# Inverse transform of a long convolution by four frequency tiles per token tile, in a fused SSM-convolution and GEGLU kernel on one core

## The chip, the core and the metric

The kernel runs on one core of a Trainium2 chip. The metric is device time of one execution in microseconds (us), the median of several runs. The core has five engines that run their own instruction streams in order: TensorE (PE, with its weight loads PEld), VectorE (DVE), ScalarE (ACT), GpSimd (POOL), and SyncE (SP), which here only issues DMAs. They wait for each other by semaphores.

## The reference

Two layers A and B, each applied twice, to 2048 tokens x 576 channels in bf16:

```python
def _A_ref(q, k, v, shift_k, ssm_k, ssm_D):
    # k_shift: causal 4-tap filter of k per channel
    kv = k_shift * v
    y = irfft(rfft(pad(kv, 2S)) * rfft(pad(ssm_k, 2S)))[:S]   # causal convolution of length S = 2048
    return q * (y + kv * ssm_D)
def _B_ref(x, w_gate, w_up, w_down):                            # 576 -> 4608 -> 576
    return (gelu(x @ w_gate) * (x @ w_up)) @ w_down

x = A_q
x = x + _A_ref(layernorm(x), A_k, A_v, ...)
x = x + _B_ref(layernorm(x), ...)
x = x + _A_ref(layernorm(x), A_k, A_v, ...)
x = x + _B_ref(layernorm(x), ...)
```

(The FFT calls are shortened here.) k, v and the filter are the same in both A layers, so y is computed once and used as a gate twice.

## The kernel before, in words

**The feed-forward part.** Tokens are cut into four chunks of 512. A *unit* is one B layer on one chunk; the eight units run in the passes [0], [1, 2], [3, 4], [5, 6], [7], and each pass goes through the 4608 hidden columns in three thirds. One unit in one third is a *visit*, so there are 24 visits, numbered here 0 to 23. A visit has a *gate/up phase* of 12 chunks (18 matmuls each, L1440, into one PSUM pair `gu`; ScalarE makes the gelu, L1444, and VectorE the product `hT`, L1445) and a *down phase* (4 token tiles of 24 matmuls, L1457, `dn`; VectorE adds the result to the residual, L1493, L1488 or L1479). Visit 0 runs in two token halves (L1365). PSUM has three rotating pairs for this (`psp`) and one for the convolution (`cps`). Chunk 2 (unit 4) needs the gate y of block 2 in visit 9, chunk 3 (unit 5) that of block 3 in visit 14, each to be ready for the next visit.

**The convolution.** The token axis is also cut into four blocks of 512. Block m's output is a sum over a of (transform of kv block a) x (transform of filter block m - a), transformed back, with half of each product sum carried over to the next block. A block has four *frequency tiles* kt of 128 and four *token tiles* mt of 128. With kt written as even or odd, and kt and kt + 2 added or subtracted, the transform splits into smaller ones.

- Forward (`quarter`, L228, pieces of two matmuls, L260): one token tile times its own two tables, ScalarE copies it out (L262), and VectorE puts the four together: `both` (L237 a float sum, L238 a float combination 2a - b), `odd` and `even` (L251, L243). Used for the filters and kv of blocks 2 and 3. The filter's pieces for block 3 wait for block 2's shifted pieces (`z_at`).
- Products (`v`, `prod`, L297 to L301) and their sums over a (`add`, L541 for the first two, L544 after that), in float, for each frequency tile and each part (real 0, imaginary 1). The float sums `zs` lie in four rotating `eo` buffers.
- `cross` (L315) adds and subtracts the sums of kt and kt + 2 into bf16 pieces (part, kt, sign); `shift` (L320) adds the former block's piece of the other part, which is the carry-over.
- `inverse` (L339): for one token tile, four pieces times four tables, in two column halves: 8 matmuls of 288 columns. ScalarE copies the tile out (L345).

The convolution's blocks 0 and 1 begin at the start, where TensorE has little else.

**What sets the order.** Everything is recorded by hand on a clock of the kernel's own (`Pace`: t.pe, t.dve, t.act, with constants such as C_PR or C_AC for costs). Between feed-forward matmuls `fill` takes VectorE steps from the queue `V` (or `U`, or the prologue steps `vq`) when their inputs are ready by that clock and they fit before a limit; `run_p` takes TensorE steps from `Pq`, in the down phase freely and in the gate/up phase only when the result is urgent. `run_loads` issues filter and kv loads on GpSimd's queue. Weight loads, and the transposes of the normalised activations `xn` into `xnT` (L1153), go through SP in the order in which the clock made them due. The instructions then run in that order on each engine, whatever the real times are.

**Both ends.** At the start, `begin` makes block 0's gate and the first activations: `head.gate` (L1291 and L1294), `head.norm` (L1244, with the statistic `rstd` from GpSimd, L1070), `head.turn` (transposes on TensorE, L1260) and `head.copy` (L1267), after which visit 0 starts. At the end, the last token tile's down product is made in two column halves, so that the first half's sum (L1466) and DMA (L1467) run while TensorE makes the second.

Of the kernel before, what the change touches and what calls it, by code (L numbers as in the profile page):

```python
# [16 lines left out]
ALU = mybir.AluOpType  # L17
F32 = mybir.dt.float32
BF16 = mybir.dt.bfloat16
# [3 lines left out]
P = 128  # L23
# [3 lines left out]
RT = BS // P  # L27
HW = 288
# [3 lines left out]
NEVER = 1e9  # L32
# [3 lines left out]
C_BF, C_TB, C_R4 = 0.41, 0.46, 0.77  # L36
C_SQ, C_TINY = 0.85, 0.6
N_KC, N_SM, N_EO, N_HR = 4, 4, 4, 3
C_AC, C_AB = 0.76, 0.76
C_TT, C_ST, C_BN, C_NORM, C_HT, C_GELU, C_EVA, C_EVD = 0.76, 0.82, 0.47, 0.62, 0.69, 0.6, 0.66, 0.76  # L40
LAG = 0.25
# [43 lines left out]
class Conv:  # L85
# [296 lines left out]
    def filt(self, b):  # L382
        nc, t, D = self.nc, self.t, self.D
        kc, own = {}, {}

        def load():
            own["t"] = self.kvp.tile([P, RT, D], BF16, tag="v", name="hT")
            nc.gpsimd.dma_start(out=own["t"][:], in_=self.Td[b].rearrange("(p i) d -> p i d", i=RT))
            own["at"] = t.pe + 9.0
        self.L.append((lambda: max(self.fwd_at.get(b - 1, NEVER), self.td_at.get(b, NEVER)), load))  # L390

        def out():
            if not kc:
                self.flush(NEVER)
                kc.update({k: self.kcp.tile([P, 2, D], BF16, tag="kc", name="hc") for k in range(RT)})
            return kc

        def seen(h):
            if h == 1:
                self.filt_at[b] = t.pe + 0.25  # L400

        def done(kt, h, when):
            if h == 1:
                for k in (kt, kt + 2):
                    self.spill(self.Hd[b][k], kc[k], when, (b, k))
        for h in range(2):
            self.Pq.extend(self.quarter(lambda: own["t"], out, h, lambda: max(own.get("at", NEVER), self.z_at[b - 1]()), seen, done))
        self.Pq.extend(self.then)
        self.then = []

    def step(self, m, kv=None, loaded=False):

        nc, D, t = self.nc, self.D, self.t
        kc, kr, hr, z, nyb, prs = {}, {}, {}, {}, {}, {}
        KTS = (0, 2, 1, 3)
# [30 lines left out]
            ready = get("k", "v") if need == "v" else get("k")  # L446
            self.V.append((ready, C_TT, run))

        pairs = [(kt, a) for kt in KTS for a in range(m + 1)]
        if m == 1:  # L450
            pairs = [(kt + (2 * e if a else 2 - 2 * e), a) for kt in range(2) for a in range(2) for e in range(2)]

# [15 lines left out]
                at[("ld", kt, a)] = t.pe + 9.0  # L468
            return run
        for kt, a in pairs:  # L470
            self.L.append((lambda a=a: max(self.hr_free[self.nhr % N_HR] if (m, a) != (1, 0) else 0.0,
                                           self.kr_free[self.nkr % 3] if a < m else 0.0,
                                           self.hd_at.get((m - a, kt), NEVER) if m - a > 1 else 0.0),
                           load(kt, a)))
# [23 lines left out]
        def out4():  # L498
            if not kc:
                self.flush(NEVER)  # L500
                kc.update({k: self.kcp.tile([P, 2, D], BF16, tag="kc", name="kc") for k in range(RT)})
            return kc

        def seen4(h):
# [10 lines left out]
        def v(kt, a, part):  # L515
            def run():
                K = kc[kt] if a == m else kr[(kt, a)][1]
                slot = None if a else self.npr % N_SM
                prs[(kt, a, part)] = (slot, self.prod(part, K, hr[(kt, a)][1], own=a > 0))
                if a == 0:  # L520
                    self.pr_free[slot] = NEVER

                def fin(when):
                    mark(("pr", kt, a, part), when + LAG)
                    if part == 1:
                        if hr[(kt, a)][0] is not None:
                            self.hr_free[hr[(kt, a)][0]] = when
                        if a < m:
                            self.kr_free[kr[(kt, a)][0]] = when
                return fin  # L530
            return run
        sums, zslot = {}, {}

        def add(kt, a, part):
            def run():
                slot, pr = prs[(kt, a, part)]
                if a == 1:
                    f, zslot[(kt, part)] = self.eo_tile("zs")
                    sums[(kt, part)] = f
                    slot0, pr0 = prs[(kt, 0, part)]  # L540
                    nc.vector.tensor_tensor(out=f[:], in0=self.halves(pr0[:]), in1=self.halves(pr[:]), op=ALU.add)  # L541
                else:
                    f = sums[(kt, part)]
                    nc.vector.tensor_tensor(out=f[:], in0=f[:], in1=self.halves(pr[:]), op=ALU.add)  # L544

                def fin(when):
                    if a == 1:
                        self.pr_free[slot0] = when
                return fin
            return run  # L550
# [13 lines left out]
        def shift(kt, part):  # L564
            def run():
                for sg in range(2):
                    z[(part, kt, sg)] = self.yb[(1 - part, kt, sg)]
                    self.shifted(nyb[(part, kt, sg)], z[(part, kt, sg)], part)
                return lambda when: mark(("z", kt, part), when + LAG)
            return run  # L570
        eo_done = get(*[("kc", kt, s, h) for kt in range(2) for s in range(2) for h in range(2)])
        for kt, a in pairs:
            for part in range(2):
                keys = [("ld", kt, a)] + ([("kc", kt % 2, s, h) for s in range(2) for h in range(2)] if a == m else [])
                self.V.append((lambda g=get(*keys), kt=kt, a=a: max(g(), 0.0 if a else self.pr_slot(),
                                                                     self.h1_at.get(kt, NEVER) if (m, a) == (1, 0) else 0.0), C_PR, v(kt, a, part)))
                if a > 0:
                    self.V.append((eo_done if a == 1 else lambda: 0.0, C_AC, add(kt, a, part)))
                if a == m and kt >= 2:
                    self.V.append((lambda: 0.0, 2 * C_AB, cross(kt - 2, part)))  # L580
                    self.V.append((lambda: 0.0, 2 * C_TB, shift(kt - 2, part)))
        for h in range(2):
            if h == 1 and m == 1:
                self.fresh = len(self.Pq)
                self.Pq.extend(self.between)
            if m > 1:
                self.Pq.extend(self.quarter(lambda: self.vt_[m], out4, h, get(("kv", h)), seen4, done4))
                continue
            for kt in range(2):
                for s in range(2):  # L590
                    self.Pq.append((lambda g=get(("kv", h)): max(g(), self.eo_slot()), 0.49, fwd(kt, s, h)))
        def inv(mt):
            def run():
                self.yb = nyb
                self.inverse(m, mt, self.terms(mt, z))
                done = t.on_act(C_EVA, t.pe + 0.98 + LAG)
                self.ps_free = done + LAG
                self.y_at[(m, mt)] = done + LAG
            return run
        zs = get(*[("z", kt, part) for kt in range(2) for part in range(2)])  # L600
        self.z_at[m] = zs
        out = [(lambda: max(zs(), self.y_used.get(m - 2, NEVER) if m > 1 else 0.0), 0.98, inv(mt), m) for mt in range(RT)]
        if m == 2:
            self.then = out
        else:
# [89 lines left out]
    def begin(self, head, tables):  # L695
# [4 lines left out]
        with ExitStack() as es:  # L700
# [134 lines left out]
                    self.prod(part, kc[kt], h0[kt], t[:])  # L835
                    A[(part, kt)] = t

            self.yb = {}

            def pair0(kt, sg):  # L840
                for part in range(2):
# [83 lines left out]
            head.norm(0)  # L925
            head.turn(0, 8)
            head.copy(0, nc.scalar.copy)
            head.gate(1, None, 0)
            head.norm(2)
            head.turn(2, 8, True)  # L930
            head.copy(2, nc.vector.tensor_copy, nc.scalar.copy)
            self.keep_y(0, 3, Y[3])
# [5 lines left out]
def ssm_geglu_kernel(ctx, tc, A_q, A_k, A_v, A_shift_k, A_ssm_k, A_ssm_D, B_x, B_w_gate, B_w_up,  # L938
# [296 lines left out]
    with tc.manual_schedule():  # L1235
# [162 lines left out]
        for wb, ph, ui, first, final in visits:  # L1398
# [50 lines left out]
                fill(t.pe + C_GU + (HURRY if hurry() else LEAD), now(), conv.left > 0)  # L1449
            for j in range(RT):  # L1450
                acc = psp.tile([P, 2, 512], F32, tag="pr", name="dn")
                xa = x_c[c][:, j, :]
                xh = xa.rearrange("p (h d) -> p h d", h=2)

                def down(fi, h):
                    at = AT0[j] if ui == 0 else j
                    nc.tensor.matmul(acc[:, h, 0:HW], lhsT=hT[:, fi, at * P:(at + 1) * P],  # L1457
                                     rhs=wd[2 * wb + fi // WT][:, fi % WT, h * HW:(h + 1) * HW],
                                     start=(fi == 0), stop=(fi == FP - 1))
                if wb == NWB - 1 and j == RT - 1:  # L1460
                    dst = out2[c * CH:(c + 1) * CH, :].rearrange("(p j) d -> p j d", j=RT)[:, j, :]
                    for h in range(2):
                        for fi in range(FP):
                            down(fi, h)
                        ob = work.tile([P, D], BF16, tag="ob", name="ob")
                        nc.vector.tensor_tensor(out=ob[:, 0:HW], in0=xh[:, h, :], in1=acc[:, h, 0:HW], op=ALU.add)  # L1466
                        nc.sync.dma_start(out=dst[:, h * HW:(h + 1) * HW], in_=ob[:, 0:HW])  # L1467
                    break
                for fi in range(FP):
# [78 lines left out]
```

## Time and profile before

| | us |
|---|---|
| median of 3 runs | 925.32 (925.19 to 926.32) |
| the profiled execution, its own time | 924.81 |
| its span in the profile | 923.0 |
| TensorE busy (matmuls) | 915.1 |
| VectorE busy | 592.1 |
| ScalarE busy | 291.6 |
| GpSimd busy | 143.4 |
| L1440, gate/up matmuls, 4968 | 541.5 |
| L1457, down matmuls, 2304 | 293.8 |
| L1445, hT on VectorE, 276 | 189.1 |

The span is what the profiler sees between the first and the last instruction; the execution's own time has 1.8 us around it. Matmuls are pipelined and a single one's length (376 ns for L1440) overlaps the next, so starts are compared, not lengths. VectorE is much fuller in the first half, where the convolution lies beside the feed-forward part: it is busy for 0.7 or more of each of the first 23 slices (a slice is a fortieth of the span) but one, and for 0.6 or less after that. TensorE is busy for 0.9 or more of every slice but the last.

### The profile page before, as it was taken

The numbers are of one execution on the slowest core, as the hardware profiler recorded it, in microseconds if no ns is written. First come the engines' busy times: TensorE is split into PE (matmuls) and PEld (weight loads), VectorE is DVE, ScalarE is ACT, GpSimd is POOL, SyncE is SP. The second block draws the span as 40 slices with busy tenths as digits, with TensorE's granted clock in tenths as the row PEclk, the third lists the DMA queues.
The fourth block names the chain that finished last, engine by engine and source line by source line (L and its number), as shares of the span: only waits on it lengthen the run. The fifth ranks groups of instructions, "written<-read, shape, count | busy, mean of one in ns | idle before, by whom it ended". The sixth has DMA issues, their size and how long they took to land.

```text
span 923.0 us, 19358 instructions
## 1 busy us (share of the span) xinstructions
PE 915.1 (99%) x8248; PEld 534.6 (58%) x8249; DVE 592.1 (64%) x1064; ACT 291.6 (32%) x538; POOL 143.4 (16%) x301
## 2 busy tenths in 40 slices
PE   9999999999999999999999999999999999999998
PEld 6786556465465565655655646646546556556555
DVE  8888977588888877888898864563333335433332
ACT  6663225433324234343123132341221224221211
POOL 2433004201113031320113101220000003000000
PEclk9999999999999999999999999999999999999999
DMA  9989977919528606963933901870820821977720
GB/s 257 344 204 255 176 185 149 257 40 250 176 89 181 199 10 107 271 129 70 264 100 82 227 31 36 164 162 1 154 78 1 155 78 21 166 176 171 141 61 26
DMA packets 128490, 130.25 MB, mean 141 GB/s; under 512 B 43538, under 2 KB 120339, under 8 KB 128404
## 3 DMA queue, kind: packets, MB, share of 16 engines
q1 hardware_dynamic: 119232, 93.47, 47.9%
q0 software_dynamic: 9168, 35.54, 11.8%
q8 instruction: 64, 1.05, 0.5%
q14 instruction: 22, 0.18, 0.1%
q10 hardware_dynamic: 4, 0.01, 0.0%
HBM read 107.76 MB, written 11.80 MB: 130 GB/s over the span
## 4 chain that ended last, share of the span: by engine, by line
PE 91%; DMA 5%; DVE 1%; SPq 1%; POOL 1%; issue 0%; ACT 0%; DVEq 0%; ACTq 0%
PE gu L1440 57%; PE dn L1457 29%; PE gu L1365 3%; DMA wgu<-in_B_w_up_dram 2%; PE cps L339 1%; DMA hn<-in_A_ssm_k_dram 1%; DMA hr<-Hd 1%; DMA Hd<-hc 1%; PE cps L260 1%; PE cps L222 1%; DMA k<-in_A_k_dram 0%; SPq L996 0%; POOL rstd L1070 0%; SPq L995 0%; ACT junk L1062 0%
## 5 line engine op out<-in xcount | busy, mean ns | idle before, releaser
L1440 PE MATMUL gu<-xnT,wgu 64*128 64x512 bf16 x4968 | 541.5, 376 | 0.4 <-DVE x_c L1488 0.4
L1440 PEld LDWEIGHTS <-wgu 64*128 64x128 bf16 x4968 | 240.6, 94 | 293.7 <-issue 7.5
L1444 ACT ACTIVATE ga<-gu 128x512 f32<-128x512 f32 x276 | 164.8, 597 | 510.5 <-PE gu L1440 501.9
L1445 DVE TENSOR_TENSOR hT<-ga,gu 128x512 bf16<-128x512 f32 x276 | 189.1, 686 | 201.7 <-ACT ga L1444 200.2
L1457 PE MATMUL dn<-wd,hT 128*128 128x288 bf16 x2304 | 293.8, 286 | 0.5 <-DVE ob L1466 0.5
L1457 PEld LDWEIGHTS <-hT 128*128 128x128 bf16 x2304 | 223.6, 98 | 66.1 <-issue 10.5
L1493 DVE TENSOR_TENSOR x_c<-x_c,dn 128x576 f32<-128x576 f32 x64 | 48.1, 752 | 57.8 <-PE dn L1457 57.6
L1054 POOL TENSOR_SCALAR nm<-s 128x1 f32<-128x1 f32 x58 | 22.3, 385 | 290.9 <-DVE x_c L1488 198.9
L1062 ACT ACTIVATE junk<-x_c,nm 128x576 bf16<-128x576 f32 x48 | 37.0, 770 | 30.2 <-POOL nm L1054 28.3
L1070 POOL TENSOR_TENSOR rstd<-ve,neghalf_t 128x1 f32<-128x1 f32 x62 | 41.5, 669 | 5.2
L467 POOL DMA_DIRECT2D hr<-Hd x32 | 17.4, 546 | 122.9 <-DVE prod L300 117.2
L262 ACT COPY eo<-cps 128x576 f32<-128x576 f32 x32 | 20.4, 637 | 36.3 <-PE cps L260 25.4
L1479 DVE TENSOR_TENSOR ob<-x_c,dn 128x576 bf16<-128x576 f32 x15 | 11.3, 753 | 29.3 <-PE dn L1457 22.7
L1365 PE MATMUL gu<-xnT,wgu 64*128 64x256 bf16 x432 | 24.7, 269 | 0.5 <-DMA wgu<-in_B_w_up_dram 0.5
L1069 POOL TENSOR_SCALAR ve<-ss 128x1 f32<-128x1 f32 x62 | 17.6, 285 | 42.0 <-ACT junk L1062 41.6
L1365 PEld LDWEIGHTS <-wgu 64*128 64x128 bf16 x432 | 21.2, 94 | 3.4 <-issue 0.7
L301 DVE TENSOR_TENSOR prod<-prod 128x576 bf16<-128x576 bf16 x48 | 22.0, 458 | 1.7
L354 POOL DMA_DIRECT2D out_dram<-ob x12 | 6.7, 555 | 95.7 <-DVE ob L1479 92.8
L544 DVE TENSOR_TENSOR zs<-zs,prod 128x576 f32<-128x576 f32 x24 | 18.1, 755 | 0.6
L541 DVE TENSOR_TENSOR zs<-sum,prod 128x576 f32<-128x576 bf16 x24 | 18.1, 755 | 0.4
L1097 DVE SCALAR_TENSOR_TENSOR x_c<-g_t,rstd,x_c 128x576 f32<-128x576 f32 x16 | 13.1, 817 | 8.2 <-POOL rstd L1070 8.1
L186 DVE TENSOR_TENSOR kvt<-k,skc 128x1152 bf16<-128x1152 bf16 x24 | 17.7, 753 | 0.2
(148 smaller groups left out, 543.7 us busy)
## 6 DMA issues: line engine op xcount, KB each, us to landing
wgu<-in_B_w_gate_dram SPq DMA_DIRECT2D x45, 576.0 KB, 5.8
wd<-in_B_w_down_dram SPq DMA_DIRECT2D x30, 864.0 KB, 7.1
wgu<-in_B_w_up_dram SPq DMA_DIRECT2D x45, 512.0 KB, 8.2
hr<-Hd POOLq DMA_DIRECT2D x32, 288.0 KB, 4.8
kr<-Kd POOLq DMA_DIRECT2D x24, 288.0 KB, 5.2
Kd<-kc POOLq DMA_DIRECT2D x12, 288.0 KB, 4.1
k<-in_A_k_dram POOLq DMA_DIRECT2D x3, 1008.0 KB, 10.5
wgu<-in_B_w_up_dram SPq DMA_DIRECT2D x45, 64.0 KB, 7.5
```

The lines of the kernel that those rows point to most:

```text
L262: nc.scalar.copy(out=A[i][:], in_=ps[:, :, 0:HW])
L301: nc.vector.tensor_tensor(out=dst, in0=pr[:, 0, :], in1=pr[:, 1, :], op=ALU.subtract if part == 0 else ALU.add)
L541: nc.vector.tensor_tensor(out=f[:], in0=self.halves(pr0[:]), in1=self.halves(pr[:]), op=ALU.add)
L1054: nc.gpsimd.tensor_scalar(out=v["nm"][:], in0=v["s"][:], scalar1=-1.0 / D, scalar2=None, op0=ALU.mult)
L1062: nc.scalar.activation(out=junk[:], in_=get_x(), func=ACT.Square, bias=v["nm"][:, 0:1], accum_out=v["ss"][:])
L1070: nc.gpsimd.tensor_tensor(out=v["rstd"][:], in0=ve[:], in1=neghalf_t[:, 0:1], op=ALU.pow)
L1365: nc.tensor.matmul(pair[:, s, e * 256:(e + 1) * 256], lhsT=w[r0:r0 + HK, k, gi * P:(gi + 1) * P], rhs=xnT[r0:r0 + HK, blk_of[k], tok], sta ...
L1440: nc.tensor.matmul(pair[:, s, :], lhsT=w[r0:r0 + HK, k, gi * P:(gi + 1) * P], rhs=xnT[r0:r0 + HK, b, :], start=(k == 0), stop=(k == NKC - 1))
L1444: nc.scalar.activation(out=ga[:], in_=pair[:, 0, :], func=ACT.Gelu_apprx_tanh)
L1445: nc.vector.tensor_tensor(out=hT[:, fi, :], in0=ga[:], in1=pair[:, 1, :], op=ALU.mult)
L1457: nc.tensor.matmul(acc[:, h, 0:HW], lhsT=hT[:, fi, at * P:(at + 1) * P], rhs=wd[2 * wb + fi // WT][:, fi % WT, h * HW:(h + 1) * HW], start ...
L1493: nc.vector.tensor_tensor(out=xh, in0=xh, in1=acc[:, :, 0:HW], op=ALU.add)
```

## The change

For blocks 2 and 3 (`quad`), the four frequency sums are put together on VectorE for each token tile before the tables, as the forward pieces already are, so that each token tile's inverse has two pieces instead of four. `halve` makes sum and difference of kt and kt + 2 in place, in float; `quart` adds or subtracts an even and an odd one into the bf16 piece of one token tile and part; `shift4` adds the carry-over per token tile. Since all four frequency sums have to be kept, those of odd kt lie in `kc` buffers instead of `eo` buffers, and for kt 3 the product with the block's own kv comes first so that its buffer is free in time. Block 1 leaves pieces of the old kind, which `convert` turns into the new kind, once. Each token tile's inverse waits for its own pieces alone. Block 2's inverse is put between the two halves of block 3's filter pieces instead of behind both. At the start, the normalisation of tile 2 stands ahead of the first half of tile 1's gate. At the end, the second column half has a PSUM tile of its own.

```diff
@@ filt
         for h in range(2):
             self.Pq.extend(self.quarter(...))
-        self.Pq.extend(self.then)
-        self.then = []
+            self.Pq.extend(self.then)
+            self.then = []
@@ step
-        pairs = [(kt, a) for kt in KTS for a in range(m + 1)]
+        quad = m > 1
+        seq = lambda kt: [m] + list(range(m)) if quad and kt == 3 else list(range(m + 1))
+        pairs = [(kt, a) for kt in KTS for a in seq(kt)]
@@ add
-                if a == 1:
-                    f, zslot[(kt, part)] = self.eo_tile("zs")
+                second = a == seq(kt)[1]
+                if second:
+                    if quad and kt % 2:
+                        self.flush(NEVER)
+                        f = self.kcp.tile([P, 2, HW], F32, tag="kc", name="zs")
+                    else:
+                        f, zslot[(kt, part)] = self.eo_tile("zs")
@@ new steps
+        def halve(kt, part):
+                lo, hi = sums[(kt, part)], sums[(kt + 2, part)]
+                nc.vector.tensor_tensor(out=hi[:], in0=lo[:], in1=hi[:], op=ALU.add)
+                nc.vector.scalar_tensor_tensor(out=lo[:], in0=lo[:], scalar=2.0, in1=hi[:], op0=ALU.mult, op1=ALU.subtract)
+        def quart(mt, part):
+                even = mt % 2 == 0
+                e, o = sums[(2 if even else 0, part)], sums[(3, part) if even else (1, 1 - part)]
+                minus = mt == 2 if even else (mt, part) in ((1, 0), (3, 1))
+                b = nyb[(mt, part)] = self.ybp.tile([P, D], BF16, tag="yb", name="yb")
+                nc.vector.tensor_tensor(out=self.halves(b[:]), in0=e[:], in1=o[:], op=ALU.subtract if minus else ALU.add)
+        def shift4(mt):
+                for part in range(2):
+                    z[(mt, part)] = self.yb[(mt, 1 - part)]
+                    self.shifted(nyb[(mt, part)], z[(mt, part)], part)
+        def convert(a, b, plus, minus):
+                lo, hi = self.yb[a], self.yb[b]
+                tmp = self.prp.tile([P, 2, D], BF16, tag="prod", name="prod")
+                nc.vector.tensor_tensor(out=tmp[:, 0, :], in0=lo[:], in1=hi[:], op=ALU.add)
+                nc.vector.tensor_tensor(out=hi[:], in0=lo[:], in1=hi[:], op=ALU.subtract)
+                nc.vector.tensor_copy(out=lo[:], in_=tmp[:, 0, :])
+                self.yb[plus], self.yb[minus] = lo, hi
@@ the queue of VectorE steps
+                if quad:
+                    if a == seq(kt)[-1] and kt >= 2:
+                        self.V.append((lambda: 0.0, 2 * C_AC, halve(kt - 2, part)))
+        if quad:
+            for mt in range(RT):
+                for part in range(2):
+                    self.V.append((lambda: 0.0, C_AB, quart(mt, part)))
+                self.V.append((lambda: 0.0, 2 * C_TB, shift4(mt)))
@@ inv
-                self.inverse(m, mt, self.terms(mt, z))
+                self.inverse(m, mt, [(self.inv_w(mt, s), z[(mt, s)]) for s in range(2)] if quad else self.terms(mt, z))
@@ begin
-            head.gate(1, None, 0)
             head.norm(2)
+            head.gate(1, None, 0)
             head.turn(2, 8, True)
@@ last token tile
+                last = wb == NWB - 1 and j == RT - 1
+                part = [acc, psp.tile([P, 2, 512], F32, tag="pr", name="dn") if last else acc]
-                    nc.tensor.matmul(acc[:, h, 0:HW], ...)
+                    nc.tensor.matmul(part[h][:, h, 0:HW], ...)
```

## The prediction on record

> **What bounds the kernel now.** I read the page first, then the chain, the waits of TensorE, its timeline around the inverses, and both ends.
>
> ```profile
> PE 915.1 (99%) x8248; PEld 534.6 (58%) x8249; DVE 592.1 (64%) x1064; ACT 291.6 (32%) x538; POOL 143.4 (16%) x301
> ...
> PE 91%; DMA 5%; DVE 1%; SPq 1%; POOL 1%; issue 0%; ACT 0%; DVEq 0%; ACTq 0%
> ```
>
> TensorE is busy 915.1 of 923.0 us and carries 91% of the chain. Its granted clock is 9 tenths or more in every slice. So a matmul taken away is worth its own length wherever nothing else becomes late. The waits (total, times, longest) say how little slack there is:
>
> ```profile
> PE xps L1260 <- DVE xn L1244: 0.8, 1, 0.8
> PE dn L1457 <- DVE ob L1466: 0.5, 1, 0.5
> ...
> PE gu L1440 <- DVE x_c L1488: 0.4, 1, 0.4
> ```
>
> Now the timeline of TensorE in visit 13 (block 3's inverse in the down phase), and after it that in visit 9 (block 2's fourth tile in the gate/up phase). First column start, second length; only starts are subtracted here, since ends are modelled.
>
> ```profile
> 550.76 1.14 PE L339 MATMUL cps<-yb,W 128*128 128x288 bf16 x8
> 551.74 1.39 PE L1457 MATMUL dn<-wd,hT 128*128 128x288 bf16 x10
> ```
>
> ```profile
> 382.81 9.89 PE L1440 MATMUL gu<-xnT,wgu 64*128 64x512 bf16 x90
> 392.62 1.16 PE L339 MATMUL cps<-yb,W 128*128 128x288 bf16 x8
> 393.71 13.77 PE L1440 MATMUL gu<-xnT,wgu 64*128 64x512 bf16 x126
> 407.42 0.42 PE L1457 MATMUL dn<-wd,hT 128*128 128x288 bf16 x2
> ```
>
> Among down matmuls, eight inverse matmuls take 551.74-550.76 = 0.98 us, 0.1225 each: no price for the interruption. Inside a gate/up phase the phase lasts 407.42-382.81 = 24.61 us, where an uninterrupted one has 23.42 in the chain: 1.19, so 0.21 on top of 0.98. I call that the switch.
>
> **The change part by part.** The execution profiled is 924.81 us (span 923.0); the sum is made against it.
>
> *The inverse.* Per token tile 8 matmuls become 4, on 2 blocks of 4 tiles: 32 matmuls x 0.1225 = **-3.92**. The order of the changed build shows the places. Before: seven of the eight groups among down matmuls, one in a gate/up phase. After: block 2's four among down matmuls of visit 8; block 3's, two among those of visit 13 and two in the gate/up phase of visit 14. A two-matmul filter piece also moves into visit 9's gate/up phase; such a piece costs there 23.89-23.42 = 0.47 (visit 5's phase, 235.84 to 259.73 in the chain), a switch of 0.22. So switches go from one to three: **+0.42**.
>
> *VectorE.* Per block it loses 8 of the 751 ns sums (L315) and gains 4 sums, 4 of the scaled kind (L238, 758 ns) and 8 sums: 8 more ops, 6.0 us a block, 12.1 in all. Block 1's pieces are converted once: 4 x (2 x 451 ns, as L320, and a copy). The trace has no 576-wide SBUF copy; 187 ns (64 wide) and 451 (a two-input op of that width) bound it. I take 250, nearer the 217 of the 256-wide copy: 4.6 us. None of it is on the path if VectorE fits. Visits 8 and 13 get most of it, since the rest of the work is moved into them. Counting the ordered ops there, visit 13 takes on 2+4+4 product ops, two first and two second sums, 4 halving and 7 quartering sums and 2 shifts, and loses 4 L315: 14.3 us by the rows' durations. It had 18.9 busy:
>
> ```profile
> 491.88:527.16 35.28, 35.28 (x314) 19.74 (x316) 31.00 (x55) 12.82 (x28) 10.06 (x19) 1.00 0.79 170
> 527.16:566.36 39.20, 39.20 (x346) 22.87 (x348) 18.91 (x31) 9.76 (x16) 1.62 (x3) 1.00 0.17 57
> ```
>
> (columns: stretch, length, then busy of PE, PEld, DVE, ACT, POOL.) Back-to-back ops start every 0.71 where one lasts 0.75, so 14.3 is about 13.5 of time: 32.4 in a visit of 39.20-2.94 = 36.3, or 0.89. Visit 12, the first row, ran at 31.00/35.28 = 0.88 with TensorE never idle. I take nothing; the third rival prices the loss of this cover.
>
> *Added waits.* Block 3's inverses now follow their shifts closely. From the start of visit 13's down phase, VectorE does the last hT (done at 1.4), a halving (2.9), a quarter, the output sum, a quarter and two shifts: 6.0. TensorE gets there after 54 matmuls, 6.6. The second tile: 9.0 against 9.8. Slack 0.6 to 0.8, cost nothing. Block 2's tiles are ready during visit 8's gate/up phase, so its wait ends earlier than before.
>
> *Queues.* Unit 5's last norm stands behind the last hT of visit 14, two chunks later than before. On SP a weight load is put ahead of three of its four pairs of transposes; it waits for the buffer that the phase's eighth chunk frees, and the second xn stands behind the ninth chunk's hT anyway. The last pair issues about 2.1 us into the down phase, takes 2 x 1.26, and lands 2.8 later: 7.4 of 11.9. POOL's filter loads only change places. I cost these at nothing; the slack of 4.5 is the cover.
>
> *The far end.* The second half's first matmul waits for a read of the same tile:
>
> ```profile
> 917.76 0.45 DVE L1466 TENSOR_TENSOR ob<-x_c,dn 128x288 bf16<-128x288 f32 x1 [0.72 <-PE dn L1457]
> ...
> 918.27 1.63 PE L1457 MATMUL dn<-wd,hT 128*128 128x288 bf16 x12 [0.55 <-DVE ob L1466]
> ```
>
> A tile of its own ends that: **-0.55**. What is late next is the second half itself; its sum and DMA follow unchanged.
>
> *The near end.* The gate step moves behind the norm of tile 2.
>
> ```profile
> 35.59 0.56 POOL L1070 TENSOR_TENSOR rstd<-ve,neghalf_t 128x1 f32<-128x1 f32 x1
> ...
> 36.89 0.81 DVE L1291 SCALAR_TENSOR_TENSOR x_c<-x_b,mv,y 128x576 f32<-128x576 bf16 x1
> 36.98 1.13 POOL L1070 TENSOR_TENSOR rstd<-ve,neghalf_t 128x1 f32<-128x1 f32 x1
> ...
> 38.15 0.58 DVE L1244 TENSOR_SCALAR xn<-x_c,nm,rstd 128x576 bf16<-128x576 f32 x1 [0.44 <-POOL rstd L1070]
> ```
>
> The norm waits for GpSimd's rstd, not for the gate step. But that rstd takes 1.13 beside the gate step and 0.56 the time before, and ends 0.41 after it. If it takes 0.56, xn starts at 37.6; the gate step then runs under the transposes, and VectorE's copy ends at 39.70 rather than 39.77, ScalarE's 0.57 earlier than 40.08. If it stays at 1.13, the gate step delays the copy to 40.24: +0.35. The chain names a weight DMA as the last releaser of the first gate/up matmul (39.87), but group 0's three loads landed 10 to 12 us after issues at 7 to 10, so I hold the copies to be last. I take **-0.2**, ends -0.3 and +0.35, by the 0.56 row.
>
> The Trainium skill, "SBUF — State Buffer", section "SBUF: two separate sides", says that VectorE ops with two SBUF inputs and GpSimd ops that read SBUF exclude each other for a whole instruction. By that rule the long rstd is the gate step's doing and this term is -0.2; without it, +0.35 and the sum 0.55 higher. The pair of rows agrees with it.
>
> **Sum:** -3.92 + 0.42 - 0.55 - 0.20 = **-4.25**, so 920.56 for an execution like the profiled one. That one lies 0.51 under the median of 925.32; I add it back: **921.1**.
>
> **Rivals.**
>
> 1. *VectorE late for the new waits.* For: four inverses have under 1 us of slack, and at the start of visit 8 (the L1488 wait above) VectorE waits in order for a chain through GpSimd. Against: block 1's inverses sat in a busy stretch without a wait. Two ops of 0.75 late, less 0.6 slack, is 0.9, at two places: +1.8, **922.9**.
>
> 2. *The gain is eaten: VectorE becomes the bound in visits 8 and 13.* For: the halvings, quarters and shifts come in dependent chains, and the order lets VectorE do little else between them. Against: 0.88 was borne without a wait. If only 0.83 can be filled, visit 13 needs 32.4/0.83 = 39.0 instead of 36.3, +2.7. Visit 8 goes by the same count from 27.87 to about 33.3, in 35.28 + 7 x 0.245 + 4 x 0.49 = 39.0; 33.3/0.83 = 40.1, +1.1. Sum +3.8: **924.9**, no change. (That the change does not do what it says is excluded by count: the build has 32 matmuls fewer.)
>
> 3. *Slower: unit 5's activations come late.* The place is the start of visit 15, the mechanism one chain: block 3's fourth inverse comes only after the seventh chunk of visit 14, then follow its copy, the last gate, three GpSimd steps and a square, and the last norm. The norm stands on VectorE ahead of the down phase's first sum (L1488), which frees a PSUM tile, and its transposes on SP ahead of a weight load. It decides from 4.5 us of slip. If the norm comes a whole down phase late, 11.9-4.5 = 7.4: **928.5**. Against: from the last gate (behind the eighth chunk's hT) to the norm there are four chunks, 7.8 us, where the same chain took 5.4 in visit 7 (337.24 to 342.63), with VectorE fuller.
>
> **How the numbers follow.** Forecast 0.76, rival one 0.11, two 0.08, three 0.05. The forecast's own ends: low 921.1-0.1 (near end) -0.4 (the L1488 wait also goes) -0.4 (no switch) -0.3 (median offset) = 919.9; high with +0.55 at the near end and the offset: 922. The range takes in the first rival and its doubt: **919.9 to 923.5**, leaving 0.13 out. About 0.2% (1.85 us) is what a measurement of this kernel can tell from no change, so faster means under 923.5: forecast and rival one, 0.87; same is rival two, 0.08; slower rival three, 0.05.
>
> **What would show it.** Right: L339 groups of four 0.49 long among down matmuls; visit 13 near 36.3 us; no wait for L1466; rstd 0.56 and an earlier first gate/up matmul; no new TensorE wait over 0.3. Wrong: a wait of L339 for shifted pieces or their copies (rival one), gate/up matmuls waiting for hT in visits 8 or 13 (two), a wait for xnT or wgu at visit 15 (three).

## The result, and the profile after

The changed kernel takes **919.99 us** (median, 919.81 to 920.6), the one before, run beside it, 925.73 (925.19 to 926.32). The ratio is 0.9939, with a 95% interval of 0.9922 to 0.9956, so the kernel is faster by 0.6%, clear of the noise. Forecast were 921.1 and a range of 919.9 to 923.5. The profiled execution took 919.96 us (span 917.8), against a sum of 920.56 for it.

In the changed kernel's listing the lines lie further down: gate/up matmuls are L1509 (before L1440), down matmuls L1528 (L1457), hT L1514 (L1445), the residual sums L1550, L1559 and L1564 (L1479, L1488 and L1493), visit 0's gate/up matmuls L1434 (L1365), the head's xn, copies and gate L1313, L1336 and L1360 (L1244, L1267 and L1291), rstd L1139 (L1070). New are `halve` (L583, L584), `quart` (L594) and `convert` (L618 to L620).

The page of the changed kernel: busy time and instructions of each engine, then the shares of the chain that ended last.

```profile
PE 911.2 (99%) x8217; PEld 530.0 (58%) x8217; DVE 607.5 (66%) x1092; ACT 291.5 (32%) x538; POOL 142.6 (16%) x301
...
PE 99%; ACT 0%; DVE 0%; DMA 0%; issue 0%; POOL 0%; DVEq 0%; ACTq 0%
```

TensorE has 31 recorded matmuls fewer (32 by the program; a record can be missing) and is busy 3.9 us less; VectorE is busy 15.4 us more. The mean granted clock is 1.0 in both profiled executions, so it plays no part in the difference.

The waits of TensorE (total us, times, longest):

```profile
PE ps L812 <- DVE full L795: 1.5, 1, 1.5
PE gu L1434 <- ACT xnT L1336: 0.8, 1, 0.8
PE ps L834 <- ACT skc L818: 0.5, 1, 0.5
PE cps L731 <- ACT kT L843: 0.3, 1, 0.3
PE xps L1329 <- DVE xn L1313: 0.2, 1, 0.2
PE ps L817 <- DMA sk<-in_A_shift_k_dram: 0.2, 1, 0.2
```

That is all that this view lists, and all of it lies in the head, ahead of visit 1 (it leaves out the shortest waits). The tail's wait for `ob` is gone, and so are two waits inside visits: the one of 0.4 for L1488 shown before, and one of 0.34 in visit 4 that I come to below. From visit 1 to the tail the view lists no wait of TensorE.

TensorE's timeline from visit 13's down phase to the end of visit 14's gate/up phase:

```profile
547.57 6.79 PE L1528 MATMUL dn<-wd,hT 128*128 128x288 bf16 x54
554.20 0.65 PE L339 MATMUL cps<-yb,W 128*128 128x288 bf16 x4
554.69 2.86 PE L1528 MATMUL dn<-wd,hT 128*128 128x288 bf16 x22
557.38 0.65 PE L339 MATMUL cps<-yb,W 128*128 128x288 bf16 x4
557.87 2.61 PE L1528 MATMUL dn<-wd,hT 128*128 128x288 bf16 x20
560.42 6.00 PE L1509 MATMUL gu<-xnT,wgu 64*128 64x512 bf16 x54
566.35 0.66 PE L339 MATMUL cps<-yb,W 128*128 128x288 bf16 x4
566.95 7.95 PE L1509 MATMUL gu<-xnT,wgu 64*128 64x512 bf16 x72
574.82 0.66 PE L339 MATMUL cps<-yb,W 128*128 128x288 bf16 x4
575.42 9.89 PE L1509 MATMUL gu<-xnT,wgu 64*128 64x512 bf16 x90
585.24 1.03 PE L1528 MATMUL dn<-wd,hT 128*128 128x288 bf16 x7
```

Four matmuls take 554.69-554.20 = 0.49 us among down matmuls, half of the 0.98 before. The gate/up phase lasts 585.24-560.42 = 24.82, which is 23.42 + 2 x 0.70: each of its two tiles costs 0.49 and a switch of 0.21, as in the forecast. No idle time stands beside any L339, so none of them waits.

Where the 4.85 us between the two profiled executions lie, by starts on TensorE:

| stretch | before | after | difference |
|---|---|---|---|
| to block 0's first inverse matmul (start of the run) | 29.52 | 29.99 | +0.47 |
| from there to visit 1 | 55.97 | 55.57 | -0.40 |
| visits 1 to 3 | 112.33 | 112.33 | 0 |
| visit 4 | 37.96 | 37.45 | -0.51 |
| visits 5 and 6 | 71.02 | 71.02 | 0 |
| visits 7 to 10 | 149.72 | 147.23 | -2.49 |
| visits 11 and 12 | 70.57 | 70.56 | -0.01 |
| visits 13 and 14 | 74.49 | 72.96 | -1.53 |
| visits 15 to 23, to the last down phase | 305.68 | 305.68 | 0 |
| last down phase to the last output sum | 12.68 | 11.97 | -0.71 |
| from there, and around the span | | | +0.33 |

The first row is scatter: it reads 29.52 to 30.45 in the traces of this study, and no edit touches what lies before it. The last row is mostly the time outside the span. That is 1.8 us in every execution of the kernel before and 2.1 in every one of the changed kernel, so it is no scatter; but e7 below, which has the same change, shows 1.8 in all ten of its executions, so the loss of 0.35 does not follow from the change as such, and what sets it stays open. Between these two rows the changed kernel gains 5.65 us. The medians stand 5.74 apart, with an interval of 4.1 to 7.2. Of visits 7 to 10, three tiles of the inverse account for 3 x -0.49, the fourth, moved from a gate/up phase to a down phase, for 0.49-1.19 = -0.70, the filter piece moved the other way for 0.45-0.245 = +0.20, and a wait gone in visit 8 for -0.53. So the inverse with its switches gives -1.97 there and -1.53 in visits 13 and 14: -3.5. Head -0.40, tail -0.71, and **-1.04 from two waits that I had left standing**.

### The profile page after: what moved, and what is told of

It reads as the page before. It is cut to its first block, busy times and chain, and to the rows that moved or that the text cites. A ratio compares the mean times of both kernels' runs of the same rounds, so it can differ in the third digit from the quotient of the medians.

```text
span 917.8 us, 19325 instructions
## 1 busy us (share of the span) xinstructions
PE 911.2 (99%) x8217; PEld 530.0 (58%) x8217; DVE 607.5 (66%) x1092; ACT 291.5 (32%) x538; POOL 142.6 (16%) x301
## 4 chain that ended last, share of the span: by engine, by line
PE 99%; ACT 0%; DVE 0%; DMA 0%; issue 0%; POOL 0%; DVEq 0%; ACTq 0%
PE gu L1509 59%; PE dn L1528 31%; PE gu L1434 3%; PE ps L211 1%; PE cps L339 1%; PE cps L260 1%; PE cps L222 1%; PE cps L211 1%; PE hps L870 0%; PE cps L731 0%; PE ps L339 0%; PE ps L222 0%; PE xps L1329 0%; PE ps L731 0%; PE ps L817 0%; DMA sk<-in_A_shift_k_dram 0%
## 5 line engine op out<-in xcount | busy, mean ns | idle before, releaser
L1509 PE MATMUL gu<-xnT,wgu 64*128 64x512 bf16 x4968 | 541.7, 376 | 0.0
L1509 PEld LDWEIGHTS <-wgu 64*128 64x128 bf16 x4968 | 239.2, 94 | 294.4 <-issue 7.4
L1514 DVE TENSOR_TENSOR hT<-ga,gu 128x512 bf16<-128x512 f32 x276 | 189.1, 685 | 195.1 <-ACT ga L1513 193.2
L1528 PE MATMUL dn<-wd,hT 128*128 128x288 bf16 x2304 | 293.3, 286 | 0.0
L1528 PEld LDWEIGHTS <-hT 128*128 128x128 bf16 x2304 | 223.5, 98 | 65.4 <-issue 9.8
L1564 DVE TENSOR_TENSOR x_c<-x_c,dn 128x576 f32<-128x576 f32 x64 | 48.1, 752 | 60.6 <-PE dn L1528 60.2
L1139 POOL TENSOR_TENSOR rstd<-ve,neghalf_t 128x1 f32<-128x1 f32 x62 | 40.8, 658 | 5.2
L1434 PE MATMUL gu<-xnT,wgu 64*128 64x256 bf16 x432 | 24.6, 269 | 0.8 <-ACT xnT L1336 0.8
L1434 PEld LDWEIGHTS <-wgu 64*128 64x128 bf16 x432 | 21.1, 94 | 3.7 <-DMA wgu<-in_B_w_up_dram 0.9
L1550 DVE TENSOR_TENSOR ob<-x_c,dn 128x576 bf16<-128x576 f32 x15 | 11.3, 753 | 18.0 <-PE dn L1528 12.6
```

The source lines that it names most:

```text
L1139: nc.gpsimd.tensor_tensor(out=v["rstd"][:], in0=ve[:], in1=neghalf_t[:, 0:1], op=ALU.pow)
L1434: nc.tensor.matmul(pair[:, s, e * 256:(e + 1) * 256], lhsT=w[r0:r0 + HK, k, gi * P:(gi + 1) * P], rhs=xnT[r0:r0 + HK, blk_of[k], tok], sta ...
L1509: nc.tensor.matmul(pair[:, s, :], lhsT=w[r0:r0 + HK, k, gi * P:(gi + 1) * P], rhs=xnT[r0:r0 + HK, b, :], start=(k == 0), stop=(k == NKC - 1))
L1514: nc.vector.tensor_tensor(out=hT[:, fi, :], in0=ga[:], in1=pair[:, 1, :], op=ALU.mult)
L1528: nc.tensor.matmul(part[h][:, h, 0:HW], lhsT=hT[:, fi, at * P:(at + 1) * P], rhs=wd[2 * wb + fi // WT][:, fi % WT, h * HW:(h + 1) * HW], s ...
L1564: nc.vector.tensor_tensor(out=xh, in0=xh, in1=acc[:, :, 0:HW], op=ALU.add)
```

## The experiments

The theory going in: the inverse's share is that of its matmuls and switches; the tail's edit is worth 0.7, which is the reported wait of 0.55 and 0.16 that the report leaves out; the waits in visits 4 and 8 went because VectorE's order shifted, not because the inverse is shorter. The rivals are named with each run. Beside e1 to e4 the kernel before took 925.42 (median of 25 executions), beside e5 to e8 925.43 (median of 19), and beside the changed kernel 925.73 (median of 4). Differences of a few tenths from the changed kernel's median are therefore read from the traces.

**The tail alone** (e1, on the kernel before):

```diff
+                last = wb == NWB - 1 and j == RT - 1
+                part = [acc, psp.tile([P, 2, 512], F32, tag="pr", name="dn") if last else acc]
-                    nc.tensor.matmul(acc[:, h, 0:HW], ...)
+                    nc.tensor.matmul(part[h][:, h, 0:HW], ...)
```

> The kernel before, with the second PSUM tile for the last column half alone. Restart theory (a wait of TensorE costs its reported length and about 0.16 us more to fill the pipeline again): from the start of the last down phase to the last sum 0.70 us less (12.58 to 11.88), all else as before. Rival (the price is the reported wait): 0.55 less. Whole time 0.1% lower or not told from before.

Measured: 924.07 (923.79 to 925.07), ratio 0.9986 [0.9977, 0.9995]. The two last sums on VectorE:

```profile
917.74 0.46 DVE L1468 TENSOR_TENSOR ob<-x_c,dn 128x288 bf16<-128x288 f32 x1 [0.71 <-PE dn L1459]
919.21 0.45 DVE L1468 TENSOR_TENSOR ob<-x_c,dn 128x288 bf16<-128x288 f32 x1 [1.01 <-PE dn L1459]
```

They start 1.47 us apart, twelve matmuls at 0.1225, so the second half runs on without a gap. The last down phase begins at 907.24 here, so the last sum starts 11.97 after it, as in the changed kernel (902.79 to 914.76), against 12.68 before: -0.71. The medians stand 1.35 apart; the interval (0.5 to 2.1 us less) takes in the 0.71, and the trace shows no more than that from this edit. The wait of 0.55 was reported from the end of the matmul ahead of it, which lies 286-122.5 ns, or 0.16 us, after the point where the next could have begun; 0.55+0.16 is 0.71. Visit 8 keeps its 40.00 us, so the tail has nothing to do with that wait. Visit 4 comes out at 37.66 without any edit near it: the wait there varies from run to run (see e4).

**The inverse with half its matmuls, and nothing else** (e2, on the kernel before):

```diff
-                self.inverse(m, mt, self.terms(mt, z))
+                self.inverse(m, mt, self.terms(mt, z)[:2] if m > 1 else self.terms(mt, z))
```

> The kernel before, blocks 2 and 3 transformed back from the first two of their four pieces; the other two are left out, so y of those blocks is partial. VectorE's work and every place stay as before. Matmul-count theory: 32 matmuls x 0.1225 = 3.9 us less, visit 8 shorter by 1.5, visit 9's gate/up phase by 0.5, visit 13 by 2.0; the waits in visits 4 and 8 (0.34 and 0.36 reported) stay. Rival (the gain comes from the new order and VectorE's new work): under 1 us less.

Measured: 921.95 (921.13 to 922.25), 0.9959 [0.9944, 0.9974]. Visit 8 is 1.47 shorter and visit 13 1.96, which is 0.49 a tile; visit 9's gate/up phase is only 0.34 shorter, since something else costs 0.17 more ahead of its inverse, which the records put down to no wait. The wait for L1488 in visit 8 stays at 0.4. Together that is -3.76 in the trace, and the medians stand 3.47 apart. A shorter inverse by itself does not remove that wait.

**The inverse at its old length in the new order** (e3, on the changed kernel):

```diff
-                self.inverse(m, mt, [(self.inv_w(mt, s), z[(mt, s)]) for s in range(2)] if quad else self.terms(mt, z))
+                self.inverse(m, mt, 2 * [(self.inv_w(mt, s), z[(mt, s)]) for s in range(2)] if quad else self.terms(mt, z))
```

> The kernel after, each of the two pieces of blocks 2 and 3 multiplied and added twice (y of those blocks is doubled): eight matmuls per token tile again, in the order of the kernel after. Matmul-count theory: 3.9 us over the kernel after, so about 1.3 to 1.8 below the kernel before. Rival (order and VectorE): within 1 us of the kernel after.

Measured: 923.81 (923.26 to 924.73), 0.9981 [0.9972, 0.9991], 3.82 above the changed kernel's median. TensorE in visit 13:

```profile
556.16 1.14 PE L339 MATMUL cps<-yb,W 128*128 128x288 bf16 x8
557.14 2.86 PE L1528 MATMUL dn<-wd,hT 128*128 128x288 bf16 x22
```

Eight matmuls take 0.98 again, visit 8 grows by 1.96, visits 13 and 14 by 0.98 each: 3.92 for 32 matmuls, as in the forecast. The two waits stay away here although the inverse has its old length. So the matmuls account for the forecast's largest term, and the waits belong to the order.

**One VectorE step whose result nothing uses** (e4, on the kernel before, at the place of the first conversion; from there on e4's line numbers are 13 higher):

```diff
+                lo, hi = self.yb[a], self.yb[b]
+                tmp = self.prp.tile([P, 2, D], BF16, tag="prod", name="prod")
+                nc.vector.tensor_tensor(out=tmp[:, 0, :], in0=lo[:], in1=hi[:], op=ALU.add)
+                nc.vector.tensor_tensor(out=tmp[:, 1, :], in0=lo[:], in1=hi[:], op=ALU.subtract)
+                nc.vector.tensor_copy(out=tmp[:, 1, :], in_=tmp[:, 0, :])
...
+        if m == 2:
+            for a, b in [((0, 0, 0), (0, 1, 0))]:
+                self.V.append((lambda: 0.0, 2 * C_TB + 0.3, idle(a, b)))
```

> The kernel before, with one step of three VectorE operations on the pieces of block 1 whose result nobody reads, at the place of the first conversion. Theory: in visit 4 the step takes the place of a product that holds VectorE until its filter DMA lands, so the 1.5 us wait of VectorE and the 0.34 us wait of TensorE for ScalarE's eo copy go, and visit 5 starts 0.5 us earlier; the whole 0.5 lower. Rival (that wait is chance in the DMA's landing): visit 4 as before.

Measured: 924.23 (923.65 to 925.08), 0.9987 [0.9978, 0.9996]: a kernel with three more VectorE ops is faster. Visit 4 is the clearest place to see why. VectorE and then TensorE there, in the kernel before:

```profile
226.09 0.76 DVE L297 TENSOR_TENSOR prod<-kr,hr 128x1152 bf16<-128x1152 bf16 x1 [1.51 <-DMA hr<-Hd]
...
227.26 0.75 DVE L1493 TENSOR_TENSOR x_c<-x_c,dn 128x576 f32<-128x576 f32 x1
```

```profile
232.48 1.14 PE L1457 MATMUL dn<-wd,hT 128*128 128x288 bf16 x8
233.97 0.41 PE L260 MATMUL cps<-v,W 128*128 128x288 bf16 x2 [0.34 <-ACT eo L262]
```

VectorE's next instruction is a product whose filter transform has not landed, and all of VectorE stands behind it for 1.51 us; the sums behind it are late, then ScalarE's copy into `eo`, then TensorE's filter piece: it starts 1.49 after the first of the eight down matmuls, which take 0.98, so 0.51 is lost, of which 0.34 is reported. In e4:

```profile
225.29 0.45 DVE L576 TENSOR_TENSOR prod<-yb 128x576 bf16<-128x576 bf16 x1
...
226.37 0.76 DVE L1506 TENSOR_TENSOR x_c<-x_c,dn 128x576 f32<-128x576 f32 x1
```

The idle step takes the product's place, the product comes later, when its data are there, and the sum starts without a wait. Visit 4 takes 37.45, as in the changed kernel, where `convert` stands at this place (224.57 to 225.85). The rival, chance in the DMA's landing, holds for the size of the wait alone: in the three traces with the old order VectorE waits here 1.51, 1.20 and 1.26 us (before, e1, e2) and visit 4 takes 37.96, 37.66 and 37.71, while in the seven traces with a step at this place it takes 37.45 or 37.46. So this wait is worth 0.20 to 0.51.

This was expected. Not expected: visit 8's wait went as well (39.45 against 39.99), since the clock shifted further steps. This wait on TensorE in the kernel before:

```profile
342.82 4.06 PE L1440 MATMUL gu<-xnT,wgu 64*128 64x512 bf16 x36
347.24 5.12 PE L1440 MATMUL gu<-xnT,wgu 64*128 64x512 bf16 x45 [0.36 <-DVE x_c L1488]
```

The 36 matmuls take 347.24-342.82 = 4.42 where their share of an unbroken phase is 3.90, so about 0.5 is lost, of which 0.36 is reported. What ends it is seen in visit 8's first microseconds on VectorE, first in the kernel before, then in e4:

```profile
343.34 0.81 DVE L1090 SCALAR_TENSOR_TENSOR g_t<-x_c,nm,y 128x576 f32<-128x576 f32 x1
345.68 0.82 DVE L1097 SCALAR_TENSOR_TENSOR x_c<-g_t,rstd,x_c 128x576 f32<-128x576 f32 x1 [1.53 <-POOL rstd L1070]
...
346.42 0.75 DVE L1488 SCALAR_TENSOR_TENSOR x_c<-dn,x_c 128x576 f32<-128x576 f32 x1
```

```profile
344.32 0.81 DVE L1103 SCALAR_TENSOR_TENSOR g_t<-x_c,nm,y 128x576 f32<-128x576 f32 x1
345.05 0.75 DVE L1501 SCALAR_TENSOR_TENSOR x_c<-dn,x_c 128x576 f32<-128x576 f32 x1
```

Before, the residual sum that frees TensorE's PSUM tile stands behind a gate step that waits 1.53 us for GpSimd; in e4, as in the changed kernel (sum at 342.98, that gate step at 345.98), the sum stands ahead of it. From visit 1 to the last down phase e4 takes 820.80 against 821.77: the two waits, -0.51 and -0.54, less 0.08 given back in visit 7. The swap of those two steps alone was not tried.

**The head's order put back** (e5, on the changed kernel):

```diff
-            head.norm(2)
             head.gate(1, None, 0)
+            head.norm(2)
```

> The kernel after, with the gate step ahead of the norm of tile 2 again. Exclusion theory: beside the gate step GpSimd's rstd takes 1.1 us instead of 0.56, the norm starts 0.6 later, and the first gate/up matmul starts about 0.3 later against block 0's inverse (10.4 instead of 10.1 us after its first matmul); whole time 0.4 over the kernel after. Rival (the first gate/up matmul waits for weights): no difference.

Measured: 920.34 (919.77 to 920.65), 0.9943 [0.9926, 0.996]; the median, 0.35 higher, cannot be told from the changed kernel's. The trace can: GpSimd's statistic there, first in the changed kernel, then in e5:

```profile
37.45 0.55 POOL L1139 TENSOR_TENSOR rstd<-ve,neghalf_t 128x1 f32<-128x1 f32 x1
...
38.03 0.58 DVE L1313 TENSOR_SCALAR xn<-x_c,nm,rstd 128x576 bf16<-128x576 f32 x1 [0.58 <-POOL rstd L1139]
...
38.73 0.81 DVE L1360 SCALAR_TENSOR_TENSOR x_c<-x_b,mv,y 128x576 f32<-128x576 bf16 x1
```

```profile
37.47 0.81 DVE L1360 SCALAR_TENSOR_TENSOR x_c<-x_b,mv,y 128x576 f32<-128x576 bf16 x1
37.55 1.14 POOL L1139 TENSOR_TENSOR rstd<-ve,neghalf_t 128x1 f32<-128x1 f32 x1
...
38.72 0.58 DVE L1313 TENSOR_SCALAR xn<-x_c,nm,rstd 128x576 bf16<-128x576 f32 x1 [0.44 <-POOL rstd L1139]
```

The same rstd takes 1.14 beside the gate step and 0.55 without it, and xn follows it in both. From block 0's first inverse matmul to the first gate/up matmul it is 10.40 us in e5 (10.39 before) and 10.10 in the changed kernel; to visit 1 it is 55.97 in e5, as before, and 55.57 in the changed kernel. So this edit is worth the head's whole 0.40. From visit 1 on e5 is the changed kernel (817.23 to the last down phase in both).

**Block 2's inverse behind both halves of the filter pieces** (e6, on the changed kernel):

```diff
         for h in range(2):
             self.Pq.extend(self.quarter(...))
-            self.Pq.extend(self.then)
-            self.then = []
+        self.Pq.extend(self.then)
+        self.then = []
```

> The kernel after, with block 2's inverse behind both halves of block 3's filter pieces. Its order puts four inverses and one filter piece into visit 9's gate/up phase, where the kernel after has one filter piece. Switch theory: four more switches at 0.21, +0.85 us over the kernel after, all of it in visits 8 and 9. Rival (a change between matmul shapes costs nothing, or the place does not matter): within 0.2.

Measured: 926.23 (924.16 to 927.25), 1.0004 [0.9995, 1.0014]. The expectation was far off. All four inverses now lie in visit 9's gate/up phase and pay their switches: from visit 8's start to visit 9's down phase it is 63.90 against 62.83, +1.07, about as expected. The rest is one wait, at visit 10:

```profile
413.86 4.82 PE L1528 MATMUL dn<-wd,hT 128*128 128x288 bf16 x38
421.55 3.83 PE L1509 MATMUL gu<-xnT,wgu 64*128 64x512 bf16 x31 [2.87 <-DMA xnT<-xn]
```

The last inverse comes after the ninth chunk of visit 9, the last gate step for unit 4 at 403.22, its norm at 409.58, the last transposes issue by 415.37, and TensorE stands for 2.87 us until they land. That is the third rival of the forecast, one pass earlier: it asked for block 3's fourth inverse, unit 5 and visit 15, and there it stays away. Here block 2's fourth inverse makes it happen at visit 10. From visit 7 to visit 10 the trace is 4.23 us longer than the changed kernel's: 1.07 for the inverses' new place and 3.16 in and behind that wait. So the place of block 2's inverse is worth 4.2 us in this trace, a little more than the shorter inverse itself. The medians stand 6.2 apart. The traced execution is one of the three that took 924.16 to 924.43; the seven others took 925.75 to 927.25, with a granted clock of 0.998 against 1.0. None of them was traced, so what costs them 2 us more is not shown.

**VectorE's new sums made twice** (e7, on the changed kernel; 16 ops of 0.75, or 12 us, which the clock doesn't know of):

```diff
                 nc.vector.tensor_tensor(out=self.halves(b[:]), in0=e[:], in1=o[:], op=ALU.subtract if minus else ALU.add)
+                nc.vector.tensor_tensor(out=self.halves(b[:]), in0=e[:], in1=o[:], op=ALU.subtract if minus else ALU.add)
```

> The kernel after, each of the 16 quartering sums made twice: 12 us more on VectorE that the kernel's clock does not know of. Cover theory: VectorE has room in most of visits 8 and 9, but block 3's first two inverses in visit 13 have 0.6 and 0.8 us of slack: TensorE waits there for the shifted pieces, 1 us and 1 us more, each with 0.16 for the restart: +2 to +2.5 over the kernel after. Rivals: VectorE is the bound in visits 8 and 13, +6 or more; VectorE has room everywhere, under 0.5.

Measured: 925.32 (924.6 to 925.88), 0.9996 [0.9987, 1.0006]: 5.3 above the changed kernel, more than twice what was expected, because visit 8 had less room than the expectation gave it. Two of TensorE's waits, and the fullest stretch of visit 8 (stretch, length, then busy of PE, PEld, DVE, ACT, POOL):

```profile
PE gu L1510 <- DVE hT L1515: 2.1, 3, 0.8
...
PE cps L339 <- DVE yb L320: 0.9, 1, 0.9
```

```profile
353.70:369.31 15.61, 12.71 (x115) 6.16 (x111) 15.37 (x28) 4.07 (x7) 0.22 (x1) 1.00 0.75 140
```

Visit 8 grows by 3.88 (gate/up and down matmuls wait for hT) and visit 13 by 1.53 (an inverse waits for its shift). VectorE is busy for 15.37 of 15.61 us, so nothing more fits. Visit 8 of the changed kernel, in three stretches:

```profile
341.65:353.35 11.70, 11.70 (x111) 5.30 (x112) 9.31 (x21) 7.05 (x15) 5.07 (x15) 1.00 0.29 58
353.35:365.06 11.71, 11.71 (x110) 5.12 (x107) 11.38 (x22) 3.58 (x6) 0.00 (x0) 1.00 0.83 142
365.06:380.61 15.55, 15.55 (x130) 12.26 (x128) 12.97 (x21) 7.66 (x12) 1.71 (x3) 1.00 0.97 177
```

In the second row VectorE is at 11.38/11.71 = 0.97 and TensorE still never idles. The cover of the extra VectorE work is there in the changed kernel, but visit 8 has used nearly all of it.

**The inverses of blocks 2 and 3 allowed two matmuls closer together** (e8, on the changed kernel):

```diff
-                self.ps_free = done + LAG
+                self.ps_free = done if quad else done + LAG
```

> The kernel after, with the inverses of blocks 2 and 3 allowed 8 instead of 10 down matmuls apart. By its order block 3's last filter piece then fits into visit 8's down phase, and visit 9's gate/up phase is not broken. Switch theory: 0.22 us less than the kernel after. Rival: no difference, or a wait of TensorE for ScalarE's copy of y, +0.2 to +0.5.

Measured: 920.08 (919.24 to 920.67), 0.9941 [0.9926, 0.9956]; the median cannot be told from the changed kernel's. The trace can:

```profile
380.94 23.48 PE L1509 MATMUL gu<-xnT,wgu 64*128 64x512 bf16 x216
404.36 1.89 PE L1528 MATMUL dn<-wd,hT 128*128 128x288 bf16 x14
```

The last filter piece now fits into visit 8's down phase, so visit 9's gate/up phase runs unbroken in 404.36-380.94 = 23.42 (23.87 in the changed kernel), and visit 8 is 0.245 longer: -0.21, the price of one switch. Among 128-row matmuls the moved piece costs just its length. The Trainium skill, "TensorEngine Tiling (Array Packing)", section "Key Properties", says that a change of the tiling mode drains TensorE. The trace agrees: only pieces put between matmuls on 64 rows pay the 0.21. No faster version than the changed kernel can be claimed from e8.

## Why the prediction was right, point by point

- **The inverse, -3.92, and the switches, +0.42:** right. The table's -1.97 and -1.53 make the -3.50 that was given; e2, e3 and e8 price the matmuls and the switch apart. (The 0.47 for a filter piece mixed times of the chain with starts; by starts it is 23.87-23.42 = 0.45.)
- **The waits in visits 8 and 4:** this is the step that failed. The sum kept the L1488 wait (its going was only an end of the range, at -0.4) and did not look at visit 4's. Both went: -0.53 and -0.51, which is most of the 1.40 between the sum's -4.25 and the 5.65 measured. (The -0.51 is that of this pair of traces; e1 and e2 put visit 4's wait at 0.20 and 0.25.) Extra VectorE work was taken to cost nothing or to lose; that it could gain, by putting an instruction in front of one that waits, was not among the cases. e4 shows it without any change to the inverse.
- **The far end, -0.55:** right in mechanism, too small; -0.71 (e1). A reported wait of TensorE was taken for its price.
- **The near end, -0.20:** right in mechanism, on the 0.56 row that it chose; the size is -0.40. To the first gate/up matmul it is -0.29, the end of the range given. A further -0.11 lies in visit 0, among its first gate/up matmuls, where one of the kernel before, and of e5, starts only behind ScalarE's copy. e5 gives back both, 0.40 in the trace. By the section of the Trainium skill that the prediction named, "SBUF: two separate sides" in "SBUF — State Buffer", the long rstd was the gate step's doing; e5's pair of rows agrees.
- **VectorE, nothing:** right, on the wrong yardstick. The mean of a visit (0.88, or 0.83 in the second rival) says little: 0.97 of 11.7 us was borne without a wait, and in e7 the limit showed as a wait for hT in the visit's middle. The count of ops was sound: 15.4 us more busy by the page, where the forecast's 12.1+4.6 = 16.7 counted overlapping starts. The copy in `convert` took 310 ns, not 250. The slack of the inverse's first two tiles in visit 13 was real: shifts end 5.6 us and TensorE comes 6.6 us into the down phase, where 6.0 and 6.6 were given. (Where the text says that the third rival prices this cover, it is the second.)
- **The queues, nothing:** right. Unit 5's last xn ends at 587.2, 2.0 into the down phase, where 2.1 was given for its transposes. They end issuing at 590.4 and land 2.8 later, and visit 15 starts at 597.1: 4 us to spare. The third rival's mechanism is real, though, as e6 shows at visit 10, so a chance for it was no idle caution.

That the total came out within the range is partly luck. All the missed sizes lay on one side, 0.16 + 0.20 + 1.04 = 1.40 of gain unforeseen, and the median ended 0.09 above the low end. The low end lay 1.2 under the forecast, of which 0.4 was for the L1488 wait, which went, and 0.4 for the case that the switches cost nothing. They did cost the 0.42, so that part of the margin stood in for visit 4's wait, which the range did not have.

## What to carry to other kernels

Where an engine runs 99% busy, count its removed instructions at their pitch and look up each remaining wait by itself, with the in-order instruction that stands ahead of the late one: any edit that moves VectorE by one instruction may remove it or make it. Judge a busy engine's room in the stretch where the work is put and by the order there, not by its mean over a visit. And where results feed a later phase through a long chain, the place of the producing step can be worth as much as what was saved on it (4.2 us in e6's trace against 3.9 here).

## What the hardware showed beyond that

- A wait reported for TensorE understates its price by 0.16 to 0.17 us in three places, since it is counted from the modelled end of the matmul ahead: 0.55 reported and 0.71 lost in the tail, 0.34 and 0.51 in visit 4, 0.36 and 0.53 in visit 8.
- The releaser that is named need not be the one that decides: the chain of the kernel before put the first gate/up matmul down to a weight DMA, while e5, with the same order at this place and the same 10.4 us, shows a wait for VectorE's copy, and an earlier norm moved the matmul by 0.3.
- Two ends that no edit touched differ between kernels: the start of block 0's inverse by up to 0.9 us from trace to trace, and the time outside the span by 0.35 us from kernel to kernel, the same in every execution of one. So the profiled pair stands 4.85 apart where the stretches between them give 5.65 and the medians 5.74. Terms of a few tenths are read from starts within a trace, not from totals.
